# A gated linear attention with two expert stages: scores by row halves of the array, the state's decay on ScalarE, other warm-up matmuls

## The chip, the cores and the metric

The kernel runs on one NeuronCore of a Trainium2 chip. The metric is device time in microseconds (us), the median over runs of the same kernel. The engines are named as the profile names them: PE is TensorE's matmul part and PEld its weight loads, DVE is VectorE, ACT is ScalarE, POOL is GpSimd, and SP issues most of the DMAs. All of these run their own instruction streams in order and wait for each other through semaphores.

## The reference

Three stages follow one another. The change lies in the first; the other two are a top-2 mixture of experts and a gated unit on 3,072 tokens of width 384.

```python
# q, k, v, alpha: (B, H, S, D) = (4, 8, 768, 48)
for t in range(S):
    state = alpha[:, :, t, :, None] * state + einsum('bhd,bhe->bhde', k[:, :, t], v[:, :, t])
    y[:, :, t] = einsum('bhd,bhde->bhe', q[:, :, t], state)
x = y.transpose(0, 2, 1, 3).reshape(B * S, H * D)
x = moe(x)      # gate + noise, two best of 8 experts, relu(x @ w1) @ w2, weighted sum
x = glu(x)      # (sigmoid(x @ w_gate) * (x @ w_val)) @ w_out
```

## The kernel before, in words

**Attention** (`attention`, lines 24 to 235) cuts the sequence into 6 chunks of 128 steps and the 8 heads into 4 pairs. That gives 24 units, one chunk of one pair of heads each (`units[u] = (chunk, pair)`), for all 4 batch entries at once. In an operand of a unit the first head of the pair lies on partitions 0 to 47 and the second on 64 to 111, so that a tile has 112 rows; its 512 columns are 4 batch entries times 128 steps. A unit goes through these steps:

- `load` brings alpha, k and q of the unit in one DMA into one of four slots `ur` (line 57, 675.5 KB).
- `st_T` makes two running products of alpha by scans on DVE (`pd`, line 96, and its inverse from the chunk's end `gi`, line 98), after ACT has put the first column in place (line 95) and with a reciprocal between them (line 97). POOL then multiplies q by `pd` in place (line 107) and k by `gi` into `kt` (line 101). ACT copies the two heads' q into `q2` (line 110), where each head has its own 512 columns and the other head's rows hold zeros.
- `st_S` computes the scores of both heads with one matmul per batch entry: 112 rows, 256 columns, the zeros in `q2` keeping the heads apart (line 124). DVE applies the causal mask in two pieces into `am` (line 126).
- `st_K` transposes `kt` on PE (line 136).
- `st_Y` adds q times the state (line 148) and the masked scores times v (line 152) into `y`; each head has its own half of the array's columns there.
- `st_U` computes the update of the state into the PSUM tile `uu` (line 167); DVE adds it to the state `st` (line 170) and multiplies the sum by the chunk's total decay (line 171).
- `st_R` transposes the result back (line 179) and, after the fourth pair of a chunk, computes gate logits (line 186, 32 matmul records) and calls the **router** of that chunk: some thirty small DVE instructions with five matmuls into the PSUM tile `rk` (lines 271 to 326), then two tables (lines 329 to 346).

The loop (lines 217 to 234) issues in iteration u the scores of unit u+1, the outputs and the update of unit u, the scans of unit u+3 and the way back of unit u-1. A scheduler that works with its own estimates orders the instructions on each engine within these dependences; the order is fixed when the kernel runs. PSUM has eight banks here: `sc` two, `tr` two, and one each for `y`, `uu`, `rk` and the table.

Eight matmuls on the identity (line 198) run before the first operands arrive. After attention come the experts (lines 452 to 500) and the gated unit (lines 691 to 762), whose products are triples of float32r matmuls (lines 414 to 416). The weights of expert 0 are loaded during attention.

## Time and profile before

| | |
|---|---|
| median of 3 runs | 1150.58 us (1149.78 to 1151.04) |
| span of the profiled execution | 1151.6 us |
| PE busy | 1100.0 us (96%) |
| DVE busy | 493.5 us (43%) |
| ACT busy | 365.5 us (32%) |
| POOL busy | 341.7 us (30%) |
| first matmul of the experts | 195.85 us into the span |

The page gives the profiled execution's own time as its span, 1151.6 us, 1.0 us above the median of the timed runs. Attention fills the first 196 us of it. The busy shares in the table are averages over the whole span and hide that the stages differ: the page's row of 40 slices and the view by windows show each stage apart.

### The profile page before, as it was taken

Reading aid. Unit: us, or ns where it says so; the run is one execution under the profiler, and the core shown is the slowest. Engines: PE = TensorE matmul, PEld = TensorE weight load, DVE = VectorE, ACT = ScalarE, POOL = GpSimd, SP = SyncE. Lnnn points to the kernel's source line nnn. Section 1 sums busy time; section 2 is a strip of 40 time slices with the busy share of each in tenths; the row PEclk is TensorE's granted clock in tenths of the full one; section 3 lists DMA queues with packets and bytes.
Section 4 is the critical chain, followed back from the end, with each engine's and each line's share of the span. In section 5 each row is a group of like instructions: output and inputs, shape, how many; then the busy total and the mean of one; then the engine's idle time right before and its main releaser. Section 6 shows DMA issues by size and latency. Waiting matters only on the chain. (4 is left out here: it accounts for less than half of the span.)

```text
span 1151.6 us, 17338 instructions
## 1 busy us (share of the span) xinstructions
PE 1100.0 (96%) x6950; PEld 1047.7 (91%) x6950; DVE 493.5 (43%) x1042; ACT 365.5 (32%) x737; POOL 341.7 (30%) x284
## 2 busy tenths in 40 slices
PE   6898879999999999999999889899999999999998
PEld 5777668999999999999999878799999999999998
DVE  8889896422222222222224779451414141413131
ACT  3443433424242424242322334221313132313131
POOL 5534451634343433333321556440202020100000
PEclk8999889999999999999999989899999999999999
DMA  9845522433333333333332554230101010000000
GB/s 240 223 148 155 165 80 77 148 93 107 91 106 89 100 95 99 96 98 97 100 93 79 172 165 134 71 97 14 49 15 48 14 49 14 28 18 4 21 1 21
DMA packets 40293, 101.25 MB, mean 88 GB/s; under 512 B 5601, under 2 KB 19329, under 8 KB 40209
## 3 DMA queue, kind: packets, MB, share of 16 engines
q1 hardware_dynamic: 33680, 80.44, 23.8%
q0 software_dynamic: 6528, 19.67, 5.8%
q8 instruction: 55, 0.90, 0.3%
q14 instruction: 30, 0.24, 0.1%
HBM read 80.42 MB, written 19.66 MB: 87 GB/s over the span
## 5 line engine op out<-in xcount | busy, mean ns | idle before, releaser
L414 PE MATMUL pg<-x2h,whi 128*128 128x384 f32 x576 | 195.1, 339 | 4.0 <-DVE sg L739 2.8
L415 PE MATMUL pg<-x2l,whi 128*128 128x384 f32 x576 | 194.9, 338 | 0.0
L416 PE MATMUL pg<-x2h,wlo 128*128 128x384 f32 x576 | 194.0, 337 | 0.0
L473 DVE SCALAR_TENSOR_TENSOR h<-ph,h 128x384 fp32r<-128x384 f32 x192 | 79.7, 442 | 258.7 <-ACT h L470 258.6
L369 POOL TENSOR_TENSOR wlo<-raw,whi 128x768 fp32r<-128x768 f32 x64 | 117.5, 1843 | 123.7 <-ACT whi L368 123.4
L416 PE MATMUL ph<-xh,wlo 128*128 128x384 f32 (+1 forms) x384 | 136.2, 355 | 0.0
L415 PE MATMUL ph<-xl,whi 128*128 128x384 f32 (+1 forms) x384 | 135.9, 354 | 0.0
L414 PE MATMUL ph<-xh,whi 128*128 128x384 f32 (+1 forms) x384 | 135.8, 354 | 0.0
L414 PE MATMUL py<-whi,h 128*128 128x384 f32 x384 | 132.3, 344 | 0.0
L470 ACT ACTIVATE h<-ph 128x448 fp32r<-128x448 f32 (+1 forms) x128 | 66.2, 518 | 207.6 <-PE ph L416 207.5
L415 PE MATMUL py<-wlo,h 128*128 128x384 f32 x384 | 128.7, 335 | 0.0
L416 PE MATMUL py<-whi,h 128*128 128x384 f32 x384 | 116.1, 335 | 0.0
L414 PEld LDWEIGHTS pg<-x2h,whi 128*128 128x128 f32 x576 | 109.3, 190 | 5.6 <-DVE sg L739 4.1
L711 POOL DMA_INDIRECT grow<-yd,row x48 | 46.9, 977 | 222.0 <-PE pt L722 174.8
L415 PEld LDWEIGHTS pg<-x2l,whi 128*128 128x128 f32 x576 | 109.4, 190 | 0.0
L416 PEld LDWEIGHTS pg<-x2h,wlo 128*128 128x128 f32 x576 | 109.3, 190 | 0.0
L368 ACT ACTIVATE gh<-sg 128x384 fp32r<-128x384 f32 x96 | 50.5, 526 | 162.2 <-DVE sg L739 162.2
L414 PE MATMUL po<-whi,gh 128*128 128x384 f32 x288 | 97.0, 339 | 4.0 <-issue 2.1
L415 PE MATMUL po<-wlo,gh 128*128 128x384 f32 x288 | 97.1, 338 | 0.2 <-POOL wlo L369 0.2
L739 DVE TENSOR_TENSOR sg<-sg,pg 128x384 f32<-128x384 f32 x96 | 52.9, 551 | 102.4 <-PE pg L416 101.5
L416 PE MATMUL po<-whi,gl 128*128 128x384 f32 x288 | 96.8, 337 | 0.0
L435 POOL DMA_INDIRECT xrow<-xd,idx x56 | 53.2, 949 | 137.0 <-PE pt L446 110.0
(168 smaller groups left out, 1885.6 us busy)
## 6 DMA issues: line engine op xcount, KB each, us to landing
ur<-in_uh_dram SPq DMA_DIRECT2D x23, 675.5 KB, 6.1
raw<-in_w1h_dram SPq DMA_DIRECT2D x32, 384.0 KB, 3.4
raw<-in_w2h_dram SPq DMA_DIRECT2D x32, 384.0 KB, 3.1
yd<-yrow SPq DMA_DIRECT2D x48, 192.0 KB, 1.9
xv<-in_vh_dram SPq DMA_DIRECT2D x6, 768.0 KB, 6.9
xd<-xr SPq DMA_DIRECT2D x6, 768.0 KB, 5.7
raw<-in_wgh_dram SPq DMA_DIRECT2D x12, 384.0 KB, 3.3
raw<-in_wvh_dram SPq DMA_DIRECT2D x12, 384.0 KB, 3.4
```

The costliest lines, as they stand in the source:

```text
L368: a = nc.scalar.activation(hi, src, AF.Copy)
L369: b = e.tensor_tensor(lo, src, hi.bitcast(FT), op=OP.subtract)
L414: nc.tensor.matmul(out, wh, mh, start=first, stop=False)
L415: nc.tensor.matmul(out, wh, ml, start=False, stop=False)
L416: nc.tensor.matmul(out, wl, mh, start=False, stop=last)
L435: nc.gpsimd.indirect_dma_start(out=x[:n], out_offset=None, in_=src, in_offset=bass.IndirectOffsetOnAxis(ap=g.idx[:n, e, a:a + 1], axis=0))
L470: a = nc.scalar.activation(h[:, :tot], p[:, :tot], AF.Relu)
L473: b = nc.vector.scalar_tensor_tensor(h[:, lo:lo + j - i], p[:, i:j], 0.0, h[:, i:j].bitcast(FT), op0=OP.max, op1=OP.subtract)
L711: nc.gpsimd.indirect_dma_start(out=r, out_offset=None, in_=src, in_offset=bass.IndirectOffsetOnAxis(ap=g.row[:, n, k:k + 1], axis=0))
L739: nc.vector.tensor_tensor(sg, sg, pp[1], op=OP.mult)
```

## The change

The scores of a unit are now eight matmuls instead of four. Each takes one head's 48 rows, which lie in the lower or the upper half of the array's rows, and 128 columns; the two heads alternate and write two PSUM tiles `s[0]` and `s[1]` in different banks (`sc` has three banks now). They read q where POOL left it, in the unit's `ur` slot, so that the copies into `q2` remain only for chunks after the first, where `st_Y` needs them, and unit 0's q is multiplied on DVE in place. A slot can be loaded again only when the scores of its unit are done; in the program text `load(u + 5)` therefore stands behind the scores of unit u+1. `am` has the heads outside the batch entries. The eighth bank comes from the router: `rk` now shares the one bank of `uu`, and the plan of the overflow (line 528) has a PSUM pool of its own. The decay of the state is four ACT instructions, one for each batch entry, with the decay as a factor per partition. The warm-up is six matmuls on the identity and thirteen on a tile of zeros in float32r, 4,480 columns together; DVE fills the tile of zeros. Comments and docstrings are gone.

```diff
@@ attention
-        nc.gpsimd.memset(q2[0], 0.0)
-        nc.gpsimd.memset(q2[1], 0.0)
...
+                qr = col(UQ)
                 if u == 0:
-                    return [e.tensor_tensor(flat(q2[0][:, j])[64 * j:64 * j + D, cs], col(UQ)[64 * j:64 * j + D],
-                                            flat(pd)[64 * j:64 * j + D, cs], op=OP.mult).ins
-                            for j, e in enumerate((nc.vector, nc.gpsimd))]
-                qr = col(UQ)
+                    return [nc.vector.tensor_tensor(qr, qr, flat(pd)[:, cs], op=OP.mult).ins]
                 q = nc.gpsimd.tensor_tensor(qr, qr, flat(pd), op=OP.mult)
-                for j in range(2):
-                    sl = slice(64 * j, 64 * j + D)
-                    nc.scalar.activation(flat(q2[u % 3][:, j])[sl], qr[sl], AF.Copy)
+                if units[u][0]:
+                    for j in range(2):
+                        sl = slice(64 * j, 64 * j + D)
+                        nc.scalar.activation(flat(q2[u % 3][:, j])[sl], qr[sl], AF.Copy)
...
         def st_S(u):
-            am = aw.tile([128, B, 2, C], FT, name="am", tag="am", bufs=2)
-            for h in range(2):
-                s = ps.tile([128, 2, 2, C], FT, name="sc", tag="sc", bufs=2)
-                for b in range(2):
-                    nc.tensor.matmul(s[:, b], KT[u][:, 2 * h + b, :], q2[u % 3][:RW, :, 2 * h + b, :],
-                                     start=True, stop=True)
-                k = nc.vector.tensor_tensor(am[:, 2 * h:2 * h + 2].rearrange("p b j t -> p (b j) t"),
-                                            s.rearrange("p b j t -> p (b j) t"), mask_b, op=OP.mult)
+            am = aw.tile([128, 2, B, C], FT, name="am", tag="am", bufs=2)
+            qt = ur[u % LB][:, UQ:UQ + BC].rearrange("p (b t) -> p b t", b=B)
+            s = [ps.tile([128, B, C], FT, name="sc", tag="sc", bufs=3) for j in range(2)]
+            for b in range(B):
+                for j in range(2):
+                    sl = slice(64 * j, 64 * j + D)
+                    nc.tensor.matmul(s[j][:, b], KT[u][sl, b, :], qt[sl, b, :], start=True, stop=True)
+            for j in range(2):
+                k = nc.vector.tensor_tensor(am[:, j], s[j], mask_b, op=OP.mult)
...
             nc.vector.tensor_tensor(s, s, o[:RW], op=OP.add)
-            nc.vector.tensor_tensor(s, s, PD[u][:, :, C - 1:C].to_broadcast([RW, B, D]), op=OP.mult)
+            for b in range(B):
+                nc.scalar.activation(s[:, b], s[:, b], AF.Copy, scale=PD[u][:, b, C - 1:C])
...
-        warm = ps.tile([128, C], FT, name="warm", tag="tr", bufs=2)
-        for _ in range(8):
-            nc.tensor.matmul(warm, ident, ident, start=True, stop=True)
+        warm = ps.tile([128, 512], FT, name="warm", tag="tr", bufs=2)
+        for _ in range(6):
+            nc.tensor.matmul(warm[:, :128], ident, ident, start=True, stop=True)
+        zero = aw.tile([128, 512], FR, name="zero", tag="am", bufs=2)
+        nc.vector.memset(zero.bitcast(FT), 0.0)
+        for w in (384, 256, 256, 256, 256, 256, 320, 320, 320, 320, 512, 512, 512):
+            nc.tensor.matmul(warm[:, :w], zero[:, :128], zero[:, :w], start=True, stop=True)
...
         st_S(0)
+        load(4)
         st_K(0, first)
-        load(4)
...
+            if u + 1 < n:
+                st_S(u + 1)
             load(u + 5)
             if p == 1 and c:
                 load_v(c + 1)
-            if u + 1 < n:
-                st_S(u + 1)
@@ router (and the same in router_fix)
-    rk = g.rps.tile([128, B, E], FT, name="rk", tag="rk", bufs=1)
+    rk = g.aps.tile([128, B, E], FT, name="rk", tag="uu", bufs=1)
```

The scheduler lays the engines' streams out anew. Three places matter below. In the rows, `st_139` to `st_142` are the states of pairs 0 to 3, and `ur_126` to `ur_129` the four slots.

On DVE, in the first chunk, the state's add and decay of units 0 and 1 stood between the scans like this before:

```order
L98 SCALAR_TENSOR_TENSOR gi<-ur_128,d_137 112x512
L170 TENSOR_TENSOR st_139<-st_139,uu 112x192
L96 SCALAR_TENSOR_TENSOR pd<-ur_129,d_136 112x512
L126 TENSOR_TENSOR am<-sc,mask 128x512
L171 TENSOR_TENSOR st_139<-st_139,pd 112x192
L97 RECIPROCAL d_138<-pd 112x4
L170 TENSOR_TENSOR st_140<-st_140,uu 112x192
L98 SCALAR_TENSOR_TENSOR gi<-ur_129,d_138 112x512
L171 TENSOR_TENSOR st_140<-st_140,pd 112x192
```

Now DVE keeps only the adds there:

```order
L96 SCALAR_TENSOR_TENSOR gi<-ur_128,d_137 112x512
L95 RECIPROCAL d_138<-pd 112x4
L168 TENSOR_TENSOR st_139<-st_139,uu 112x192
L96 SCALAR_TENSOR_TENSOR gi<-ur_129,d_138 112x512
L168 TENSOR_TENSOR st_140<-st_140,uu 112x192
```

and ACT has the decays, in order with the copies that other engines wait for:

```order
L153 ACTIVATE xt<-y 128x512
L170 ACTIVATE st_139<-st_139,pd 112x48 x4
L372 ACTIVATE whi<-raw 128x768
L153 ACTIVATE xt<-y 128x512
L372 ACTIVATE whi<-raw 128x768
L170 ACTIVATE st_140<-st_140,pd 112x48 x4
```

The decays have left DVE, and on ACT they stand between the copies of `y` and the splits of the weights.

On DVE, where the router of the first chunk runs, the adds of units 6 and 7 (pairs 2 and 3 of the second chunk) stood among the router's instructions, one of them ahead of the two that read `rk`:

```order
L170 TENSOR_TENSOR st_141<-st_141,uu 112x192
L326 TENSOR_TENSOR wts<-w,wts 128x4
L171 TENSOR_TENSOR st_141<-st_141,pd 112x192
L96 SCALAR_TENSOR_TENSOR pd<-ur_128,d_135 112x512
...
L311 TENSOR_TENSOR m<-m,rk 128x32 x2
L313 TENSOR_REDUCE rank<-m 128x8
...
L170 TENSOR_TENSOR st_142<-st_142,uu 112x192
```

Now, since `uu` and `rk` are one bank, the add of unit 5 (pair 1) already comes behind the readers of `rk`:

```order
L315 TENSOR_TENSOR m<-m,rk 128x32 x2
L317 TENSOR_REDUCE rank<-m 128x8
...
L346 TENSOR_TENSOR ohh<-ohe,ids 128x224
L168 TENSOR_TENSOR st_140<-st_140,uu 112x192
L344 TENSOR_TENSOR ohe<-codes,code 128x224
L346 TENSOR_TENSOR ohh<-ohe,ids 128x224
L94 SCALAR_TENSOR_TENSOR pd<-ur_127,d_136 112x512
```

The updates of units 5, 6 and 7, pairs 1 to 3 of the second chunk, now all stand behind the readers of `rk`; before, only that of unit 7 did.

On SP the loads of units 4 and 5 stood between those of expert 0's weights:

```order
L395 DMA raw<-in_w1h_dram 128x768
L57 DMA ur_126<-in_uh_dram 112x1544
L395 DMA raw<-in_w1h_dram 128x768 x2
L57 DMA ur_127<-in_uh_dram 112x1544
```

Now all three weight loads go first:

```order
L399 DMA raw<-in_w1h_dram 128x768 x3
L57 DMA ur_126<-in_uh_dram 112x1544
L57 DMA ur_127<-in_uh_dram 112x1544
```

Two weight loads have moved ahead of unit 4's operands.

## Rows read from the trace of the kernel before

**Rows 1.** The page, busy tenths of PE and DVE in 40 slices of the span.
```profile
PE   6898879999999999999999889899999999999998
...
DVE  8889896422222222222224779451414141413131
```
**Rows 2.** By windows of the attention stage: us, busy time (instructions) of each engine, PEclk, DMA.
```profile
core 0: us, PE busy (x) PEld busy (x) DVE busy (x) ACT busy (x) POOL busy (x), PEclk, DMA share, GB/s
15.00:50.00 35.00, 30.17 (x278) 23.10 (x278) 33.02 (x44) 17.73 (x38) 18.99 (x14) 0.90 0.97 248
50.00:78.00 28.00, 25.85 (x301) 21.72 (x298) 24.88 (x64) 12.11 (x27) 9.21 (x7) 0.98 0.49 144
78.00:110.00 32.00, 27.36 (x299) 23.48 (x300) 28.99 (x66) 14.33 (x31) 14.46 (x11) 0.91 0.51 158
110.00:145.00 35.00, 28.98 (x313) 24.79 (x307) 31.96 (x67) 15.03 (x33) 18.00 (x13) 0.90 0.55 170
145.00:175.00 30.00, 22.81 (x255) 19.24 (x254) 29.64 (x67) 9.25 (x21) 14.38 (x10) 0.89 0.26 77
```
**Rows 3.** DVE by line and form, 15 to 178 us: busy us, mean ns | idle before, releaser.
```profile
L96 DVE TENSOR_TENSOR_SCAN pd<-ur,d 112x512 f32<-112x512 f32 x22 | 30.3, 1379 | 1.8 <-ACT d L95 1.1
L126 DVE TENSOR_TENSOR am<-sc,mask 128x512 f32<-128x512 f32 x43 | 28.5, 669 | 1.0 <-PE sc L124 0.7
L171 DVE TENSOR_TENSOR st<-st,pd 112x192 f32<-112x192 f32 x20 | 16.4, 818 | 0.3
L170 DVE TENSOR_TENSOR st<-st,uu 112x192 f32<-112x192 f32 x20 | 6.8, 340 | 6.9 <-PE uu L167 6.9
```
**Rows 4.** Line 171 alone: ns min/median/max, first and last start.
```profile
L171 DVE TENSOR_TENSOR st<-st,pd x20: 326/360/2823, 23.6 to 172.9; 112x192 f32<-112x192 f32 x20
```
**Rows 5.** DVE in order of time, the longest decay and the longest scan: start us, us.
```profile
143.34 2.82 DVE L171 TENSOR_TENSOR st<-st,pd 112x192 f32<-112x192 f32 x1
150.42 3.74 DVE L96 TENSOR_TENSOR_SCAN pd<-ur,d 112x512 f32<-112x512 f32 x1
```
**Rows 6.** PE in order of time in one unit at the full clock: start us, us.
```profile
65.19 0.60 PE L179 MATMUL tr<-ident,xt 128*128 128x128 f32 x4
65.63 1.89 PE L124 MATMUL sc<-q,kt 112*128 112x256 f32 x8
67.45 0.44 PE L148 MATMUL y<-q,st 128*64 128x128 f32 x4
67.72 0.39 PE L152 MATMUL y<-am,xv 128*64 128x128 f32 x4
67.94 0.39 PE L148 MATMUL y<-q,st 128*64 128x128 f32 x4
```
**Rows 7.** ACT by line, 0 to 330 us: small copies, busy us, mean ns.
```profile
L95 ACT ACTIVATE d<-ur 112x4 f32<-112x4 f32 (+1 forms) x25 | 5.1, 207 | 45.7 <-DVE pd L96 16.8 <-DMA ur<-in_uh_dram 15.5 <-issue 13.2
...
L190 ACT ACTIVATE ls<-tr 128x128 f32<-128x128 f32 x6 | 1.6, 272 | 10.8 <-PE tr L186 10.8
```
**Rows 8.** PE in order of time at the start: start us, us [idle before, releaser].
```profile
2.07 3.41 PE L198 MATMUL warm<-ident 128*128 128x128 f32 x16 [2.07 <-POOL ident masks.py:199]
7.78 1.48 PE L124 MATMUL sc<-q,kt 112*128 112x256 f32 x4 [2.30 <-DVE kt L101]
...
12.30 2.05 PE L124 MATMUL sc<-q,kt 112*128 112x256 f32 x4 [2.66 <-DVE d L97]
```
**Rows 9.** ACT in order of time at the start: first columns of units 1 and 2.
```profile
10.37 0.21 ACT L95 ACTIVATE d<-ur 112x4 f32<-112x4 f32 x1 [7.07 <-DMA ur<-in_uh_dram]
...
16.79 0.21 ACT L95 ACTIVATE d<-ur 112x4 f32<-112x4 f32 x1 [1.49 <-DMA ur<-in_uh_dram]
```
**Rows 10.** By windows at the start (columns as in Rows 2).
```profile
10.00:15.00 5.00, 2.42 (x7) 1.65 (x8) 4.36 (x6) 1.71 (x4) 3.08 (x6) 0.50 1.03 254
15.00:20.00 5.00, 5.00 (x35) 3.76 (x36) 3.74 (x6) 1.63 (x5) 1.29 (x2) 0.64 1.04 260
```
**Rows 11.** PE in order of time where the experts begin.
```profile
178.63 1.99 PE L124 MATMUL sc<-q,kt 112*128 112x256 f32 x8
...
195.85 0.42 PE L414 MATMUL ph<-xh,whi 128*128 128x384 f32 x1
196.11 0.34 PE L415 MATMUL ph<-xl,whi 128*128 128x384 f32 x1
196.28 0.34 PE L416 MATMUL ph<-xh,wlo 128*128 128x384 f32 x1
```
**Rows 12.** Loads of line 57, from issue to landing.
```profile
DMA to landing us min/median/max: 4.6/6.1/15.1
```

More of the change, by code (lines that the diff above doesn't have):

```diff
@@ L33, in attention @@
             tc.tile_pool(name="aps", bufs=1, space=PSUM) as ps:
-        ident = g.ident
+        ident, g.aps = g.ident, ps
         LB = 4
@@ L151, in st_Y @@
                     h0 = b * HD + (2 * p + j) * D
-                    nc.tensor.matmul(y[64 * j:64 * j + 64, b], vt[:, h0:h0 + 64], AM[u][:, b, j, :],
+                    nc.tensor.matmul(y[64 * j:64 * j + 64, b], vt[:, h0:h0 + 64], AM[u][:, j, b, :],
                                      start=not c, stop=True, skip_group_check=True)
@@ L205, in attention @@
         with tc.issue_after(g.after_T):
-            nc.gpsimd.memset(q2[2], 0.0)
+            for t in q2:
+                nc.gpsimd.memset(t, 0.0)
             for p in range(NP):
@@ L352, in router_fix @@
     E = g.E
-    pc = g.rps.tile([128, E], FT, name="pc", tag="rk", bufs=1)
+    pc = g.aps.tile([128, E], FT, name="pc", tag="uu", bufs=1)
     nc.tensor.matmul(pc, g.ones, g.run, start=True, stop=True)
@@ L526, in overflow_plan @@
     TT = lambda *a, **k: nc.vector.tensor_tensor(*a, **k)
-    pc = g.rps.tile([128, E], FT, name="oc", tag="rk", bufs=1)
-    nc.tensor.matmul(pc, g.ones, g.run, start=True, stop=True)
     cnt = t("cnt", [128, E])
-    TT(cnt, pc, g.roff, op=OP.add)
+    with tc.tile_pool(name="ops", bufs=1, space=PSUM) as ops:
+        pc = ops.tile([128, E], FT, name="oc")
+        nc.tensor.matmul(pc, g.ones, g.run, start=True, stop=True)
+        TT(cnt, pc, g.roff, op=OP.add)
     one = t("one", [128, E])
```

## The prediction

> **What bounds the kernel now.** I read the page's slices first, to see which engine is full in which stage. PE is full from the seventh slice on, in the experts and the gated unit; in the first six, 173 us, DVE is the fuller of the two almost throughout [rows 1]. The change touches the attention stage and the router in it, so what it is worth is read there. The windows of that stage give, from 15 to 175 us, 33.02 + 24.88 + 28.99 + 31.96 + 29.64 = 148.5 us of DVE in 160 us, 93%. PE has 30.17 + 25.85 + 27.36 + 28.98 + 22.81 = 135.2 us there, 84%, part of it at a granted clock that drops to half (means of 0.89 to 0.98). ACT has 68.4 us, 43% [rows 2]. So DVE sets the pace and PE follows closely; ACT has room. DVE's own idle time confirms it: before its longest groups it waits 1.8 us and 1.0 us in total, and only the add of the state's update, line 170, has a real wait, 6.9 us in 20 instructions, for PE [rows 3].
>
> Behind the attention stage the experts' products begin at 195.85 us and follow each other every 0.17 us [rows 11], with PE full up to slice 20 [rows 1]. Nothing there can take up time that attention gives back, so what is saved before 196 us comes off the end, one for one. The profiled span of 1151.6 us stands 1.0 us above the median of the runs shown; I take the sum off the median, 1150.58 us. About 0.2%, 2.3 us, is what a measurement can tell from no change.
>
> **The change, part by part.**
>
> *The decay leaves DVE.* Line 171 costs DVE 16.4 us in 20 instructions, 818 ns each [rows 3]. The median is only 360 ns, the longest 2,823 ns [rows 4]: the same operation on the same shape, so the rest is waiting inside the instruction while something else is being served. The part that surely goes is 20 x 0.36 = 7.2 us. The other 16.4 - 7.2 = 9.2 us are stalls, and a stall can pass to the next instruction. A scan has stalled for 3.74 us where its mean is 1.38 us [rows 3, 5], so scans are not safe from it. I take half of the stalls as gone: 7.2 + 4.6 = **11.8 us gained**, with 7.2 and 16.4 us as the ends.
>
> *The decay arrives on ACT.* It is four instructions of 112 x 48 a unit, 80 in all. The nearest ACT rows are a copy of 112 x 4 at 207 ns and one of 128 x 128 at 272 ns [rows 7]; between them I take 240 ns, 80 x 0.24 = 19 us. ACT has 160 - 68.4 = 91.6 us idle in the stage [rows 2], and three units' copies into `q2` leave it, so in total it fits. But ACT works in order: a decay waits for DVE's add, which waits for PE's update, and the first columns for the scans and the copies of `y` queue behind it. DVE waits for such a first column when it is late, 1.1 us in the stage now [rows 3]. I take 1 us lost; the ends are 0 and a wait like those of line 170, 6.9 us.
>
> *The scores.* Now a unit's scores start at 65.63 us and the next group at 67.45 us: 1.82 us for eight records [rows 6]. The array is already split by columns in `y`: there four records, two matmuls of 128 columns for each half, start every 0.22 us (67.72 to 67.94) [rows 6]. One such matmul alone streams half as many columns as a score matmul now, which is 1.82 / 4 = 0.455 us, so about 0.23 us; two in 0.22 us means that the halves really run together. If the row halves do likewise, a unit's scores take 4 x 0.22 = 0.9 us. If they stream one after the other, 8 x 0.23 = 1.8 us, as now. In between stands the weight load: each score matmul loads 128 columns anew, and the transposes at 65.19 us, which also load 128 columns each, need 0.44 us for four, 0.11 us a load, for operands that stream little [rows 6]. Sixteen loads (two records a matmul) in a row would be 1.76 us, in pairs 0.88 us. I take the middle of 0.9 and 1.8, 1.3 us, so 0.5 us of PE a unit.
>
> The Trainium skill (TensorE: Matmul & The Clock Gate, section LDWEIGHTS) has the load's time go by columns alone, not by rows, and lets it overlap with matmuls of another row group; that agrees with 0.11 us for 128 columns, and no run here shows whether two loads overlap. By serial loads the scores would gain 0.06 us a unit, and the sum below would lose its PE term.
>
> In the DVE-bound stretch the 22 units' 0.5 us, 11 us of PE, are hidden behind DVE and I count them as nothing. They do keep PE below DVE: without them PE's 135.2 us would stand against DVE's 148.5 - 11.8 = 136.7 us. From 175 to 196 us PE is the bound, with the last two units' scores in it, the first of them at 178.63 us and 1.99 us long [rows 11]. There 2 x 0.65 = **1.3 us gained**, with 0 and 2.2 us as the ends.
>
> *q read from the slot.* A slot is now free only when the unit's scores are done, not when ACT has copied q. A load takes 6.1 us from issue to landing in the median, 15.1 us at most [rows 12]. Scans run two units or more ahead of scores, and a slot serves every fourth unit, so two units' time is left, about 2 x 160 / 22 = 14.5 us. That covers the median. At the start DMA is full (0.97 of it, 248 GB/s, 15 to 50 us [rows 2]), and two weight loads of 0.39 MB now go ahead of unit 4's load: 0.79 MB / 248 GB/s = 3.2 us later. I take **1 us lost** for units 4 to 8, with 0 and 3.2 us as the ends. Later loads are hidden.
>
> *`rk` in the bank of `uu`.* Unit 5's update now waits until DVE has read the ranks. DVE still has the rest of the router and a table to do between the two, as the order shows, and PE's outputs of units 6 to 8 stand ahead of that update on PE. I cost it at nothing; what hides it is that DVE work. Without the cover each of five rounds would cost one wait like the present ones of line 170, which I bound below among the rivals.
>
> *The start.* Warm-up before: 16 records in 3.41 us from 2.07 us, then PE idles 2.30 us until DVE has `kt` at 7.78 us [rows 8]. Now it is 12 records, 2.6 us, and 4,480 columns; a 384-column product takes 0.17 us at the full clock [rows 11], so 2.0 us, or 4.0 us at half. It ends between 6.7 and 8.7 us, against 7.78 us. The second half of the first scores stands at 12.30 us, behind DVE's chain for unit 1 [rows 8], whose operands land only at 10.37 us, and unit 2's at 16.79 us [rows 9]. PE ran at a granted 0.50 and 0.64 in these ten microseconds [rows 10]; a fuller warm-up may raise that, but DMA sets the pace there. The memset of the zeros (nearest: 112 x 512) and the q product on DVE also end in that wait. Nothing, with 1 us either way.
>
> The sum: -11.8 + 1 + 1 - 1.3 = -11.1 us, 1150.6 - 11.1 = **1139.5 us**. Most of the ends together give 1134 to 1146 us for this case.
>
> **The rivals.**
>
> *Both engines give way (more gain).* If the stalls vanish with line 171 (16.4 us) and the faster scores also end DVE's waits for PE (6.9 us), with 1.3 us at the end: 1150.6 - 24.6 = 1126 us; half way there 1132 us. For it: PE and DVE are both near full. Against: a scan stalls as well [rows 5].
>
> *A wait takes the place.* The bank shared by `rk` and `uu`, or a decay late on ACT, holds DVE up once or twice a chunk. The price: 6.9 us of waits before line 170 fell mostly on few instructions; a wait of about 2 us a unit in the 5 chunks that update, 5 to 6 of them, is 10 to 12 us and eats the gain: 1139.5 + 10 to 12, with 1.5 us of play 1148 to 1153 us. For it: the updates of units 5 to 7 are bunched behind the router. Against: DVE has work in between.
>
> *The row halves do not run together (slower).* Streams and loads then add up: 8 x 0.23 + 16 x 0.11 = 3.6 us a unit against 1.82 us. PE would gain 22 x 1.8 = 39 us of work in a stretch of 160 us that has 135.2 us of it [rows 2]. It decides from 160 - 135.2 = 25 us on, 1.1 us a unit. Beyond that PE is the bound: 39 - 25 = 14 us, and 4 us for the last two units, 1168 us; with loads partly hidden 1154 us. For it: no row here shows row halves. Against: column halves do run together.
> The Trainium skill (TensorEngine Tiling (Array Packing), section Tiling Modes, Key Properties) says that a change of tiling mode drains TensorE, which speaks against this change, since scores now have a mode of their own. In the trace the first group of `y` behind the scores takes 0.27 us and the next 0.22 us, so a drain of about 0.05 us; that agrees in kind and is small.
>
> **How the numbers follow.** Forecast 0.62, more gain 0.12, a wait in its place 0.12, slower 0.14. Faster by over 0.2%: 0.62 + 0.12 and a sixth of the third case, 0.76; within 0.2%: the rest of that case, 0.10; slower 0.14. The range 1128 to 1151 us holds the forecast, most of the greater gain and half of the third case, about 0.8.
>
> **What would show it.** Right: line 170 on ACT at some 240 ns, no multiply of the state on DVE, DVE still over 90% busy up to some 165 us, scores near 1.3 us a unit, the first expert product at some 185 us. Wrong: DVE idle before adds or masks with PE or ACT as the releaser, score groups of 3 us, first columns waiting for DMA, or a first expert product at 196 us or later.

## The result and the profile after

The changed kernel takes 1164.91 us (1163.57 to 1166.47), the kernel before, timed beside it, 1150.5 us (1149.78 to 1151.04): a ratio of 1.0116 [1.0094, 1.0139] (of the times, with its 95% interval in brackets, here and below), 14 us slower. I had forecast 1139.5 us and a range up to 1151 us; sign and range are both wrong.

The profiled execution has a span of 1162.6 us, 11 us more than the profiled one of before; the timed medians lie 14 us apart. The page's slices of PE and DVE answer to [rows 1], and the granted clock is shown beside them:

```profile
PE   7898788899999999999999889899999999999998
...
DVE  7788896422222222222223869642414141413131
...
PEclk8789888999999999999999999999999999999999
```

The experts begin at 206.84 us, 11 us later than in [rows 11], and the rest of the span behind them is as long as before (955.8 us either way). So what the two profiles differ in happens in attention:

```profile
206.84 0.42 PE L418 MATMUL ph<-xh,whi 128*128 128x384 f32 x1
207.10 0.34 PE L419 MATMUL ph<-xl,whi 128*128 128x384 f32 x1
```

The windows of that stage, columns as in [rows 2]:

```profile
15.00:50.00 35.00, 29.90 (x285) 26.37 (x286) 28.34 (x36) 16.98 (x45) 20.53 (x18) 0.70 0.77 210
50.00:78.00 28.00, 26.29 (x326) 22.86 (x328) 19.93 (x58) 14.23 (x41) 6.41 (x5) 0.93 0.43 124
78.00:110.00 32.00, 28.55 (x353) 24.49 (x352) 28.22 (x63) 17.60 (x48) 14.60 (x10) 0.93 0.48 147
110.00:145.00 35.00, 28.52 (x315) 24.75 (x314) 30.51 (x62) 19.30 (x48) 21.56 (x13) 0.84 0.55 169
145.00:175.00 30.00, 26.36 (x288) 22.06 (x287) 29.72 (x53) 13.95 (x32) 23.79 (x14) 0.86 0.48 149
```

DVE is busy for 136.7 us of these 160 us instead of 148.5 us; PE for 139.6 instead of 135.2 us although its scores are shorter, at a lower clock in four of the five windows. (The windows are the same times, not the same work: the changed kernel has 11 us more of attention behind them.) DVE by line and form, 15 to 178 us, and the decay's line on ACT alone, which answer to [rows 3, 4]:

```profile
L96 DVE TENSOR_TENSOR_SCAN gi<-ur,d 112x512 f32<-112x512 f32 x22 | 43.7, 1986 | 1.1
L94 DVE TENSOR_TENSOR_SCAN pd<-ur,d 112x512 f32<-112x512 f32 x22 | 37.0, 1682 | 4.3 <-ACT d L93 3.5 <-ACT st L170 0.8
L125 DVE TENSOR_TENSOR am<-sc,mask 128x512 f32<-128x512 f32 x42 | 27.5, 674 | 9.3 <-PE sc L123 7.8 <-PE y L150 1.4
```
```profile
L170 ACT ACTIVATE st<-st,pd x80: 317/319/336, 24.0 to 189.3; 112x48 f32<-112x48 f32 x80
```

The decay's 16.4 us have left DVE, and its scans have grown by as much, from 64.0 us (30.3 for `pd` [rows 3] and 33.7 for `gi`) to 80.7 us. That is not one passing into the other: where the decay alone is moved, the scans grow far less, to 70.8 us in decay_only, and from 69.8 to 72.5 us between own_bank_decay_back and after_own_bank (all below). DVE also waits 9.3 us before masks, where it was 1.0 us. The scores themselves did what they should, a unit in 1.09 us at the full clock against 1.82 us [rows 6]; PE in order of time:

```profile
87.89 1.16 PE L123 MATMUL sc<-ur,kt 48*128 48x128 f32 x16
88.98 0.33 PE L191 MATMUL tr<-ident,ls 128*128 128x128 f32 x1
```

### The profile page after: what moved, and what is told of

It reads as the page before. It is cut to its first block, busy times and chain, and to the rows that moved or that the text cites. A ratio compares the mean times of both kernels' runs of the same rounds, so it can differ in the third digit from the quotient of the medians.

```text
span 1162.6 us, 17796 instructions
## 1 busy us (share of the span) xinstructions
PE 1109.5 (95%) x7151; PEld 1060.3 (91%) x7151; DVE 485.6 (42%) x1023; ACT 380.5 (33%) x811; POOL 349.9 (30%) x282
## 3 DMA queue, kind: packets, MB, share of 16 engines
q1 hardware_dynamic: 33680, 80.44, 23.1%
## 5 line engine op out<-in xcount | busy, mean ns | idle before, releaser
L373 POOL TENSOR_TENSOR wlo<-raw,whi 128x768 fp32r<-128x768 f32 x64 | 121.1, 1899 | 126.4 <-ACT whi L372 126.0
L418 PE MATMUL ph<-xh,whi 128*128 128x384 f32 (+1 forms) x384 | 136.7, 357 | 0.0
```

Of the source, the lines that this page charges most:

```text
L373: b = e.tensor_tensor(lo, src, hi.bitcast(FT), op=OP.subtract)
L418: nc.tensor.matmul(out, wh, mh, start=first, stop=False)
```

## The experiments

Two figures are worked out for every kernel from windows of 1 us, from 10 us to the first product of the experts. *Idle* is the time in which PE was not busy. *Slow* is PE's busy time times one minus the granted clock: what its work took beyond what it takes at the full clock. They carry an error of a few us, since some matmul records are missing. Four profiles (decay_only, no_decay, scores_split, rows_after_start) hold no record of the clock before 21.4, 18.5, 17.2 and 21.2 us, and the windows print 1.00 there. Their matmuls say otherwise: four score matmuls of 112 rows and 256 columns take 2.04 us in this stretch of rows_after_start, as at 0.50 in the kernel before [rows 8, 10], and 1.13 us later at the full clock.

```profile
12.78 2.04 PE L125 MATMUL sc<-q,kt 112*128 112x256 f32 x4 [2.57 <-DVE d L97]
```

So this stretch is counted at half the clock for these four. The ratio is to the kernel before, timed beside each (its medians there: 1150.5 to 1151.7 us).

| kernel | us | ratio [95%] | experts begin | slow | idle |
|---|---|---|---|---|---|
| before | 1150.5 | 1 | 195.85 | 13.2 | 27.4 |
| after | 1164.9 | 1.0116 [1.0094, 1.0139] | 206.84 | 27.2 | 30.1 |
| bank_only | 1164.8 | 1.0115 [1.0098, 1.0132] | 209.10 | 11.7 | 39.2 |
| rows_only | 1153.7 | 1.0028 [1.0014, 1.0042] | 200.58 | 30.6 | 28.2 |
| decay_only | 1152.3 | 1.0014 [1.0004, 1.0025] | 196.40 | 14.4 | 26.5 |
| after_own_bank | 1152.0 | 1.0002 [0.9989, 1.0014] | 194.63 | 19.7 | 27.9 |
| after_decay_back | 1172.9 | 1.0189 [1.0171, 1.0207] | 215.72 | 29.1 | 37.2 |
| own_bank_decay_back | 1152.0 | 1.0001 [0.9991, 1.0011] | 193.64 | 23.6 | 24.5 |
| after_pd6 | 1161.0 | 1.0081 [1.0058, 1.0104] | 203.47 | 22.3 | 24.6 |
| after_router_later | 1160.5 | 1.0085 [1.0062, 1.0108] | 201.89 | 27.1 | 25.8 |
| no_decay | 1155.2 | 1.0024 [1.0003, 1.0045] | 196.35 | 17.9 | 25.3 |
| own_bank_no_decay | 1163.5 | 1.0088 [1.0062, 1.0114] | 203.63 | 28.1 | 32.1 |
| own_bank_pd6 | 1161.4 | 1.0094 [1.0070, 1.0117] | 200.92 | 27.5 | 28.1 |
| decay_only_pd6 | 1151.6 | 1.0008 [0.9993, 1.0023] | 198.95 | 12.0 | 32.5 |
| own_bank_kt_dve | 1151.3 | 1.0001 [0.9987, 1.0016] | 195.70 | 28.7 | 23.1 |
| own_bank_fill2 | 1155.8 | 1.0041 [1.0018, 1.0064] | 198.86 | 19.4 | 24.5 |
| own_bank_fill4 | 1176.6 | 1.0217 [1.0179, 1.0255] | 215.66 | 20.1 | 30.7 |
| own_bank_decay_back_fill2 | 1167.4 | 1.0138 [1.0115, 1.0161] | 208.74 | 23.9 | 27.6 |
| scores_split | 1152.8 | 1.0017 [1.0007, 1.0026] | 193.85 | 10.8 | 27.3 |
| rows_after_start | 1154.5 | 1.0021 [1.0008, 1.0035] | 198.72 | 24.9 | 29.0 |

### The parts alone, and without one part

**rows_only**: the kernel before with `st_S` by row halves (and `am` ordered by head for it), q from `q2`, `rk` in its own bank. Here and below `...` stands for code that is left out.

```diff
-                    nc.tensor.matmul(s[:, b], KT[u][:, 2 * h + b, :], q2[u % 3][:RW, :, 2 * h + b, :], ...)
+                    nc.tensor.matmul(s[j][:, b], KT[u][sl, b, :], q2[u % 3][sl, j, b, :], ...)
```


> The kernel before with the scores by row halves alone: q still read from the copies in q2, masks by head, two banks for sc, the router's own bank, decay on DVE, old warm-up. In its order on DVE 23 of 45 neighbouring scans have no mask between them (13 before, 25 after). Order theory (scans that stand side by side meet POOL's products and get longer; 33 of 46 met one after the change, 20 before): most of the loss is here already, 1157 to 1165 us, over 28 scans that meet a product. Bank theory (rk in the bank of uu makes the wait): no loss, 1140 to 1150 us. Decay theory (the decay comes late on ACT): no loss, 1140 to 1150 us.

**decay_only**: the kernel before with the four ACT instructions in place of line 171.

> The kernel before with the decay on ACT alone. Order on DVE: 13 of 45 scan pairs without a mask, as before. Order theory: the decay's stalls go only in part to scans, 1142 to 1149 us, about 20 scans that meet a product. Bank theory: the same, 1140 to 1149 us. Decay theory: the loss is here, 1155 to 1165 us, with DVE or PE waiting for line 171 on ACT.

**after_decay_back**: the changed kernel with line 171 back on DVE.

> The changed kernel with the decay back on DVE. 25 of 45 scan pairs without a mask, as after. Order theory: not faster than after, 1162 to 1172 us. Bank theory: as after or slower, 1162 to 1172 us. Decay theory: back to 1145 to 1152 us.

**after_own_bank**: the changed kernel with two banks for `sc` instead of three, and the third given to `rk`, `pc` and `oc`.

```diff
-    rk = g.aps.tile([128, B, E], FT, name="rk", tag="uu", bufs=1)
+    rk = g.rps.tile([128, B, E], FT, name="rk", tag="rk", bufs=1)
-            s = [ps.tile([128, B, C], FT, name="sc", tag="sc", bufs=3) for j in range(2)]
+            s = [ps.tile([128, B, C], FT, name="sc", tag="sc", bufs=2) for j in range(2)]
```


> The changed kernel with the router's own bank again and therefore two banks for sc. 18 of 45 scan pairs without a mask. Order theory: between the two, 1152 to 1160 us, since the order lies between the two. Bank theory: the whole loss goes, 1138 to 1150 us. Decay theory: little change, 1158 to 1166 us.

Measured: 1153.7, 1152.3, 1172.9 and 1152.0 us. The bank is the one part that costs much: 12.9 us between after and after_own_bank. But after_own_bank only comes back to the kernel before and brings none of the gain that the bank theory left over, and decay_only gains nothing either. rows_only loses 3 us, less than the order theory gave. The decay theory falls: decay_only takes 1152.3 us and not 1155 to 1165, and putting the decay back makes the changed kernel slower. rows_only, decay_only and after_decay_back lie outside every range that was given, after_own_bank at the lower end of the order theory's. No part gains anything by itself. The decay's move is worth 8.0 us where the bank is shared (1172.9 to 1164.9) and nothing where it is not (own_bank_decay_back, below).

**bank_only** puts `rk` and `pc` into the bank of `uu` in the kernel before and changes nothing else.

```diff
-    rk = g.rps.tile([128, B, E], FT, name="rk", tag="rk", bufs=1)
+    rk = g.aps.tile([128, B, E], FT, name="rk", tag="uu", bufs=1)
```


> The kernel before with rk and the table's counts in the bank of uu and nothing else changed: the decay stays on DVE, the scores as they were. Chain theory: the shared bank costs by itself what it cost in the changed kernel, about 13 us, 1159 to 1166 us, with scans standing behind the routers. Rival, it only costs because the decay on ACT comes behind it, or because PE and DVE changed their order around the new scores: under 4 us, 1149 to 1155 us.

1164.8 us: the shared bank costs 14 us alone, with the decay and the scores as they were. PE's slow time does not rise (11.7 us); its idle time does, by 11.8 us. So this part is a wait, as the chain theory has it; the next section follows it. In the changed kernel the same bank shows up in other columns: against after_own_bank the idle time is 2.2 us higher and the slow time 7.5 us. Nor do the parts add up: after_decay_back, which differs from bank_only in the row halves, q's product, the loads and the warm-up, takes 8 us more than it. No run says which of these costs that.

### The way of the bank's cost

The next four pieces are DVE in order of time around the first router (start us, us, then the idle time before and its releaser). They show scans (not all of them), the state's add and decay, and the first reader of `rk`; `...` stands for what is left out. The kernel before:

```profile
47.27 1.23 DVE L96 TENSOR_TENSOR_SCAN pd<-ur,d 112x512 f32<-112x512 f32 x1
...
54.04 0.36 DVE L170 TENSOR_TENSOR st<-st,uu 112x192 f32<-112x192 f32 x1 [2.53 <-PE uu L167]
54.43 0.36 DVE L171 TENSOR_TENSOR st<-st,pd 112x192 f32<-112x192 f32 x1
54.88 1.22 DVE L96 TENSOR_TENSOR_SCAN pd<-ur,d 112x512 f32<-112x512 f32 x1
...
61.69 1.22 DVE L96 TENSOR_TENSOR_SCAN pd<-ur,d 112x512 f32<-112x512 f32 x1
...
66.77 0.28 DVE L311 TENSOR_TENSOR m<-m,rk 128x32 f32<-128x32 f32 x2
```

bank_only:

```profile
48.74 1.72 DVE L98 TENSOR_TENSOR_SCAN gi<-ur,d 112x512 f32<-112x512 f32 x1
...
61.03 0.28 DVE L311 TENSOR_TENSOR m<-m,rk 128x32 f32<-128x32 f32 x2
...
64.26 0.35 DVE L170 TENSOR_TENSOR st<-st,uu 112x192 f32<-112x192 f32 x1 [0.60 <-PE uu L167]
64.83 0.35 DVE L171 TENSOR_TENSOR st<-st,pd 112x192 f32<-112x192 f32 x1
65.40 1.22 DVE L96 TENSOR_TENSOR_SCAN pd<-ur,d 112x512 f32<-112x512 f32 x1
```

The changed kernel:

```profile
55.10 1.66 DVE L96 TENSOR_TENSOR_SCAN gi<-ur,d 112x512 f32<-112x512 f32 x1
...
65.77 0.28 DVE L315 TENSOR_TENSOR m<-m,rk 128x32 f32<-128x32 f32 x2
...
68.55 0.36 DVE L168 TENSOR_TENSOR st<-st,uu 112x192 f32<-112x192 f32 x1 [0.16 <-PE uu L165]
...
70.44 1.23 DVE L94 TENSOR_TENSOR_SCAN pd<-ur,d 112x512 f32<-112x512 f32 x1 [0.81 <-ACT st L170]
71.70 0.18 DVE L95 RECIPROCAL d<-pd 112x4 f32<-112x4 f32 x1
71.99 2.11 DVE L96 TENSOR_TENSOR_SCAN gi<-ur,d 112x512 f32<-112x512 f32 x1
```

after_own_bank:

```profile
56.08 0.35 DVE L168 TENSOR_TENSOR st<-st,uu 112x192 f32<-112x192 f32 x1
...
57.77 1.23 DVE L94 TENSOR_TENSOR_SCAN pd<-ur,d 112x512 f32<-112x512 f32 x1 [0.46 <-ACT st L170]
...
60.30 0.27 DVE L315 TENSOR_TENSOR m<-m,rk 128x32 f32<-128x32 f32 x2
...
64.80 1.22 DVE L94 TENSOR_TENSOR_SCAN pd<-ur,d 112x512 f32<-112x512 f32 x1
```

Before, the add of unit 5 comes at 54.04 us, and scans run beside the router, at 54.88 and 61.69 us; in after_own_bank it is much the same. With the shared bank, in bank_only and in the changed kernel, unit 5's add comes only behind the reader of `rk`, at 64.26 and 68.55 us, and no scan runs for 14.9 and 13.7 us. It is the same at the second and the third router: 12.2 and 13.7 us without a scan in bank_only, 12.5 and 15.0 us in the changed kernel, while the longest such stretch is 6.8 us before and 6.7 us in after_own_bank. The bank goes from tile to tile in the order of the program text, and there the router of the first chunk stands ahead of unit 5's update. A scan into `pd` needs a buffer; there are four, and the scan of unit 9 gets that of unit 5, which is free when unit 5's decay has read it. So the chain is: router, update, decay, buffer, scan. POOL, which waits for the scans, stands idle for 13.58 us meanwhile in the changed kernel:

```profile
71.75 1.27 POOL L103 TENSOR_TENSOR ur<-ur,pd 112x512 f32<-112x512 f32 x1 [13.58 <-DVE pd L94]
```

Two runs change this chain and leave the bank shared. **after_pd6** gives `pd` six buffers:

```diff
-            pd = aw.tile([RW, B, C], FT, name="pd", tag="pd", bufs=4)
+            pd = aw.tile([RW, B, C], FT, name="pd", tag="pd", bufs=6)
```


> The changed kernel with six buffers for the running product pd instead of four; rk still shares the bank of uu. Chain theory (router holds the update, the update holds the decay, the decay holds the pd buffer, and the scans of four units later stand behind it): with two more buffers the scans no longer stand behind the router, POOL's idle stretch of 13.6 us beside the first router is gone, and most of the 13 us comes back: 1148 to 1156 us. Rival, the waits for the bank hurt by themselves (PE's updates, the adds, the order of the router's instructions, of masks and scans): no more than a third comes back, 1160 to 1166 us.

**after_router_later** issues a chunk's router one unit later in the text, behind the next unit's update (the list `late` holds it until then):

```diff
...
             st_U(u)
+            if late:
+                on_round(*late.pop())
...
```


> The changed kernel, rk still in the bank of uu, but the router of a chunk stands one unit later in the program text, behind the update of the next unit (not for the last chunk and one other). The bank goes to rk and uu in the order of the text, so the update of the second pair of the next chunk no longer waits for the router. Theory that the 13 us are the updates which stand behind the router (three a round): one of three is taken out of three of the rounds, so 3 to 6 us come back, 1158 to 1162 us. Rival, the loss comes from the bank's turn as such or from the bunched scans whatever is ahead: 1163 us or more.

They measured 1161.0 and 1160.5 us, about 4 us back each. after_router_later is as expected: with one of three updates ahead of the router in three of the rounds, about a third of the loss is gone. after_pd6 falls to the rival by its time, no more than a third comes back. But its trace shows the chain still whole: two more scans into `pd` pass beside the first router (51.99 and 58.77 us), and then the scan of unit 11, whose buffer is now that of unit 5, stands behind the same decay.

```profile
60.31 2.27 DVE L96 TENSOR_TENSOR_SCAN gi<-ur,d 112x512 f32<-112x512 f32 x1
...
73.33 1.23 DVE L94 TENSOR_TENSOR_SCAN pd<-ur,d 112x512 f32<-112x512 f32 x1 [0.35 <-ACT st L170]
```

At the three routers 10.8, 13.0 and 16.6 us pass without a scan there, and 11.2, 12.2 and 11.0 us in after_router_later. So it is shown that the shared bank costs 13 to 14 us and that updates behind the router cost time (three of the twelve moved ahead, 4 us back). That the `pd` buffers are the whole way from the late update to the end is argued from the order: no run has enough buffers to take that link out.

### What the decay is worth

**no_decay** leaves the decay out altogether, in the kernel before (a constant factor in the copy `km` keeps the state small); **own_bank_no_decay** does so in after_own_bank, where the decay's lines are those on ACT.

```diff
-            nc.vector.tensor_tensor(s, s, PD[u][:, :, C - 1:C].to_broadcast([RW, B, D]), op=OP.mult)
-            nc.scalar.activation(km, o[:, :, :RW], AF.Copy)
+            nc.scalar.activation(km, o[:, :, :RW], AF.Copy, scale=1e-6)
```


> The kernel before without the state's decay on any engine (left out: the multiply of the state by the chunk's decay; in its place the copy into km carries a constant factor 1e-6, about the mean decay of a chunk, so that the state stays small). This is the most that taking the decay off DVE can ever give, with no late decay on ACT. My prediction's premise, DVE's time in this stage comes off the end one for one: 1134 to 1144 us (7.2 to 16.4 us faster). Rival, the stage's pace comes from the chain through scans, POOL's products, scores, masks, outputs and router, not from DVE's fullness: 1147 to 1152 us.

> The changed kernel with rk in its own bank and without any decay (left out as in no_decay). With the decay on ACT this kernel took 1152.0 us, and DVE waited 9.0 us for ACT to release pd. Theory that this late release takes the gain: 1141 to 1147 us. Rival, scans that stall beside POOL's products and the order of the work take it: 1149 to 1153 us.

**own_bank_decay_back** is after_own_bank with line 171 back on DVE.

> The changed kernel with rk in its own bank and the decay back on DVE: what is left of the change is the row halves, the q product in the slot, the order of the loads and the warm-up. It completes the table bank times decay. If the decay's move is worth as much with its own bank as with the shared one (8 us): 1158 to 1162 us. If it is worth only what it was alone (nothing): 1151 to 1155 us, near rows_only's 1153.7 us.

**own_bank_pd6** and **decay_only_pd6** are after_own_bank and decay_only with six `pd` buffers.

> The changed kernel with rk in a bank of its own (scores in two banks) and six buffers for pd. Before this run, with four buffers, DVE waited 9.0 us in six scans for ACT's decay to release pd. Theory that the late decay on ACT takes what its leaving DVE gives: these waits go and the time falls by 4 to 9 us, 1143 to 1148 us, faster than the kernel before. Rival, DVE is not what limits any more (PE at a lower clock, or scans that stall beside POOL's products): the waits move elsewhere and the time stays within 2 us of 1152 us.

> The kernel before with the decay on ACT alone and six buffers for pd. In the run with four buffers, 1152.3 us, DVE waited 6.8 us in eight scans for ACT to release pd. Late-decay theory: 1144 to 1149 us. Rival, PE as the limit beside DVE: 1150 to 1153 us, with PE busier and DVE's idle time put down to PE in place of ACT.

This is what fells my main term. With no decay on any engine the kernel before takes 1155.2 us, not 1134 to 1144 us, and not even the rival's 1147 to 1152. own_bank_decay_back equals after_own_bank (1152.0 us both), and decay_only_pd6, 1151.6 us, falls to its rival by the time, though PE is not busier there, as the rival had it (156.4 us up to the experts, 159.9 in decay_only). Where `rk` has its own bank, moving the decay, putting it back and leaving it out all give the same time or a longer one. What becomes of the time on DVE is seen in no_decay, 15 to 178 us, first before, then no_decay (columns as in [rows 2]), then what DVE waits for there (us in total, times, longest):

```profile
15.00:178.00 163.00, 138.17 (x1465) 114.93 (x1466) 148.66 (x305) 70.22 (x151) 75.05 (x53) 0.92 0.56 160
```
```profile
15.00:178.00 163.00, 139.53 (x1457) 118.11 (x1454) 141.99 (x285) 69.93 (x150) 81.50 (x53) 0.91 0.53 158
DVE am L126 <- PE sc L124: 5.7, 6, 1.3
DVE pd L96 <- ACT d L95: 3.5, 5, 1.1
DVE gi L98 <- POOL kt L101: 2.8, 4, 0.9
```

Of the 16.4 us DVE gives back 6.7; the rest returns as longer scans and router instructions. And the 6.7 us become waiting, for PE, ACT and POOL; in the kernel before DVE waits 0.7 us for these scores and 1.1 us for the first columns [rows 3]. The late release of `pd` by ACT is real, in after_own_bank:

```profile
DVE pd L94 <- ACT st L170: 9.0, 6, 2.5
```

(us in total, times, longest), but taking it away with more buffers did not help: own_bank_pd6 has no such wait and is 9 us slower, own_bank_no_decay 11 us; both lie outside what either theory gave. So the theory of the late release finds no support. In own_bank_no_decay and own_bank_pd6 the scans may run further ahead, and PE's slow time is 8 us higher than in after_own_bank; why is not settled. Every edit here also makes the scheduler lay the streams out anew, and no run holds the order fixed: 9 us for two more buffers shows how much that can move, so a time that an edit failed to save is weaker evidence than the waits in its trace.

### What a scan waits for

In the rows of after above, the scan at 70.44 us takes 1.23 us, and the one at 71.99 us takes 2.11 us. POOL's product ran from 71.75 to 73.02 us: 1.03 us of waiting for its end and 1.2 us of scan are about that. Counted in the timelines of DVE and POOL, a scan that overlaps a product on POOL (of attention, or of the experts' weights, `wlo`) by less than 0.3 us takes 1.22 us on average, in after as in before; one that overlaps more takes 2.07 us in after (33 of 46 scans) and 1.77 us in before (20 of 46). The masks never stall (654 to 693 ns for all 48 of after); they read PSUM and one tensor in SBUF. The Trainium skill (SBUF — State Buffer, section Who interferes with whom) states that DVE and GpSimd share a port pair as an exclusive lock; the trace agrees for scans, which read two SBUF tensors, 2.07 us against 1.22 us.

**own_bank_kt_dve** puts the products `kt` of all units on DVE.

```diff
-                e = nc.vector if u < 2 else nc.gpsimd
+                e = nc.vector
```


> The changed kernel with rk in its own bank and the product kt of all units on DVE instead of POOL. DVE gets 20 products of some 0.69 us more, 14 us. Contention theory (a scan takes 1.2 us alone and about 2 us beside a product on POOL): scans beside POOL's products fall from 24 to about 12 of 46, the scans' total falls by about 10 us and pays for most of it: 1150 to 1156 us with a mean scan under 1.45 us. Rival, scans are long for another reason: their mean stays at 1.65 us and the time rises by the products, 1160 to 1168 us.

DVE by line and form, 15 to 178 us:

```profile
L96 DVE TENSOR_TENSOR_SCAN gi<-ur,d 112x512 f32<-112x512 f32 x22 | 44.7, 2032 | 0.2
L94 DVE TENSOR_TENSOR_SCAN pd<-ur,d 112x512 f32<-112x512 f32 x22 | 28.8, 1309 | 1.9 <-issue 1.7
L99 DVE TENSOR_TENSOR kt<-ur,gi 112x512 f32<-112x512 f32 x22 | 17.2, 781 | 0.2
```

The time, 1151.3 us, is inside the contention theory's range, but not for its reason: the mean scan is 1.67 us, not under 1.45. 14 scans meet work on POOL instead of 24, yet take longer (2.71 us), and the scans' sum stays at 73.5 us against 72.5 us. The timelines say why. Ten of the 14 meet only the product of q, and these take 2.07 us on average, as in after. The other four meet splits of the experts' weights on POOL (`wlo`, 128 x 768), one or two in a row, and take 2.58, 4.01, 4.85 and 5.77 us, 17.2 us together; the four that meet splits in after_own_bank take 10.3 us. The longest:

```profile
57.72 5.77 DVE L96 TENSOR_TENSOR_SCAN gi<-ur,d 112x512 f32<-112x512 f32 x1
```
```profile
57.60 1.27 POOL L103 TENSOR_TENSOR ur<-ur,pd 112x512 f32<-112x512 f32 x1 [4.56 <-PE uu L165]
58.83 3.58 POOL L373 TENSOR_TENSOR wlo<-raw,whi 128x768 fp32r<-128x768 f32 x2
```

The contention is as the theory has it, and half of the scans are free of it; what it left out are the splits, which now follow the product of q at once and hold scans just as well. DVE is busy for 149.0 us from 15 to 178 us against 142.6 in after_own_bank, so 16.5 us of products more are 6.3 us net, and they cost nothing in total, as the 6.7 us less of no_decay gained nothing.

### The clock of TensorE

In the table the six kernels with the old scores have 10.8 to 17.9 us of slow time, and the fourteen with row halves 19.4 to 30.6 us. Every timed execution has its mean granted clock on record too: the medians are 0.978 to 0.982 for the six, and 0.962 to 0.972 for the fourteen. Row halves save PE 8 to 13 us of work at the full clock (145.2 us before, 131.8 in rows_only, 137.0 in after_own_bank, each to the experts), and 6.5 to 17 us go into a lower clock.

**scores_split** cuts each old score matmul into two of 128 columns, on all 112 rows; **rows_after_start** is rows_only with the old scores for units 0 to 4.

```diff
-                    nc.tensor.matmul(s[:, b], KT[u][:, 2 * h + b, :], q2[u % 3][:RW, :, 2 * h + b, :],
...
+                    for j in range(2):
+                        nc.tensor.matmul(s[:, b, j], KT[u][:, 2 * h + b, :], q2[u % 3][:RW, j, 2 * h + b, :],
...
```


> The kernel before with each score matmul (112 rows, 256 columns) cut into two of 128 columns, still on all 112 rows with the zeros in q2. It has the row halves' number of matmuls and weight loads without the row halves. If the half-filled rows are what keeps TensorE's clock at half for longer: PE's slow loss stays at 10 to 15 us as in the five kernels with the old scores, 1149 to 1154 us. Rival, it comes from the many short matmuls or from the new order: slow loss of 19 us or more, or over 1156 us.

> rows_only (1153.7 us, slow loss 30.6 us), with the scores of units 0 to 4 in the old form of 112 rows. In rows_only TensorE stays at half clock up to about 36 us though PE is full from 16 us on; in the kernel before it is at the full clock from 18.6 us. If row halves keep the clock down: it is up at about 19 us again, the slow loss falls to 18 to 24 us, and the time to 1145 to 1151 us, which would beat the kernel before if below 1148. Rival, the slow start there is chance of the order: no change, 1152 to 1156 us.

One window of rows_only, then of rows_after_start (columns as in [rows 2]):

```profile
20.00:26.00 6.00, 6.00 (x52) 5.67 (x52) 5.14 (x8) 1.84 (x4) 5.25 (x3) 0.50 1.04 266
```
```profile
20.00:26.00 6.00, 6.00 (x58) 4.71 (x58) 6.00 (x8) 2.27 (x4) 2.54 (x2) 1.00 1.05 267
```

PE is full in both, at 1.2 GHz with row halves and, from 21.2 us on, at 2.4 GHz with the old scores. In rows_only the clock stays at 0.50 from 26 to 36 us as well, with PE busy for 8.06 of 10 us. scores_split has as many matmuls as the row halves and the lowest slow time of all, 10.8 us; over its ten executions the median of the mean clock is 0.982, as before, and 0.966 in rows_only. So the clock goes with the row halves, not with the number of matmuls; that is shown. What it is about them is not. But rows_after_start, with 6 us less slow time than rows_only, takes 1154.5 us: its slow time, 24.9 us, stays just above what was expected, and its gain is not there. It is no test of the clock alone: the old scores of five units are also 3 us more work for PE, so that PE's busy time up to the experts only falls from 162.4 to 159.7 us. The clock is where the saved work went; no run raised it without adding work.

**own_bank_fill2**, **own_bank_fill4** and **own_bank_decay_back_fill2** put two or four idle matmuls ahead of each unit's scores, on the tile of zeros, which is kept for them. The edit, simplified:

```diff
+            for _ in range(2):
+                nc.tensor.matmul(s[0].rearrange("p b t -> p (b t)"), g.zero[:, :128], g.zero, start=True, stop=True)
```


> The changed kernel with rk in its own bank and, ahead of each unit's scores, two idle matmuls of 512 columns on zeros, written into the score tile and overwritten. Clock theory (what the row halves save on PE goes back into TensorE's clock, which stands at half for 20 us of PE's time more than needed in this kernel, 13 us in the kernel before): PE's slow loss falls from 19.7 to under 13 us, and although 48 matmuls cost 10 us of PE at 0.21 us each, the time does not rise by that: 1146 to 1153 us. Rival, the pace is PE's work itself or the chain through DVE and POOL, and the clock follows from it: 1156 to 1164 us.

> The same with four idle matmuls a unit, 20 us of PE at the full clock. Clock theory: slow loss under 8 us, time 1148 to 1158 us. Rival: about 20 us more than 1152 us, 1166 to 1174 us.

> own_bank_decay_back (1152.0 us; slow loss 23.6 us, idle 24.5 us of PE up to the experts) with two idle matmuls a unit. Clock theory: slow loss under 14 us, 1143 to 1151 us, and it would be the candidate that beats both kernels. Rival as for own_bank_fill2: 1156 to 1164 us.

1155.8, 1176.6 and 1167.4 us, with slow times of 19.4, 20.1 and 23.9 us, as without them. The idle matmuls do not lower the slow time, and they hide in part at best: 4, 25 and 15 us more than without them for 10, 20 and 10 us of added PE work. The clock theory asked for a slow time under 13, 8 and 14 us, so it falls; the rival's ranges are not hit either (one time lies just below, two above). PE's time does count, then.

## Why the prediction was wrong

- **"`rk` in the bank of `uu` ... I cost it at nothing; what hides it is that DVE work."** This step failed. What I put at nothing costs 13 to 14 us (bank_only, after_own_bank). The order that I showed had the sign of it: three adds behind the readers of `rk`. I looked at who works meanwhile (DVE has a router to run) and not at what the late update holds up in turn: the decay, the `pd` buffer, the scans, POOL, and in the trace 12.5 to 15.0 us without a scan at each of three routers. My second rival had the cause and nearly the size, 10 to 12 us, at a chance of 0.12, but as waits of 2 us a unit and set against a gain that does not exist.
- **"What is saved before 196 us comes off the end, one for one", and "DVE sets the pace".** Wrong, and it carried the whole gain. no_decay takes all of line 171 away, which leaves DVE 6.7 us less busy, and gains nothing; own_bank_kt_dve adds 16.5 us of products, 6.3 us net, and loses nothing. The 93% of [rows 2] held 9.2 us of stalls in line 171, at 1.22 us a scan 10 us in the scans (64.0 - 44 x 1.22), and 10 us in two router instructions (lines 315 and 322 take 1423 and 1520 ns on average in the kernel before, 165 and 164 ns in after), so it did not say that DVE was full.
- **The decay leaves DVE, 11.8 us.** The sure 7.2 us and half the stalls were to go. Line 171 is gone, and my warning that a stall can pass on was right: where the decay alone is moved (decay_only), the scans grow by 6.8 us and DVE's busy time from 15 to 178 us falls by 5.7 us, less than even the sure 7.2. But it was not the share that failed: none of what DVE gave back came off the end.
- **The decay on ACT, 240 ns.** It takes 319 ns, 25.5 us in all. It fitted, as I said; DVE waits 0.8 us for it in the changed kernel, 9.0 us in after_own_bank, against my 1 us.
- **The scores, 1.3 us a unit.** 1.09 us, better than my middle. The halves run together, and so do their weight loads: 16 loads in a row would be 1.76 us by my price. The Trainium skill (TensorE: Matmul & The Clock Gate, section LDWEIGHTS) lets a load run ahead of matmuls where the row groups do not conflict; here the 16 loads of a unit start in pairs, one of each half, a pair every 0.11 us (87.89 to 88.67 us), so loads overlap with each other as well. My rival of halves that do not run together is refuted, though the time fell into its range: right sign, wrong reason. What I did not think of is that PE's clock answers to the form of the scores.
- **q from the slot, and the start.** Unit 4's first scan starts at 30.39 us against 27.81 us, but after_own_bank, which has the same loads in the text, has it at 28.39 us and loses nothing. With the new warm-up the clock is 0.83 from 10 to 15 us against 0.50 [rows 10], and down again afterwards (0.50 from 15 to 20 us, 0.64 before); the second half of the first scores came at 12.39 us, before at 12.30 us [rows 8]. Nothing, as forecast for the start; no run takes these two out alone.

Two of my signs of being wrong came true: DVE waits before masks for PE (7.8 us, where it was 0.7), and the first expert product is later than 196 us.

What sets the 186 us of attention once the bank is put right stays open. PE idles for 23 to 32 us there in nearly every kernel; less work on PE, on DVE or on both does not shorten it, more on PE lengthens it. No version ran that beats the kernel before; after_own_bank, own_bank_decay_back, own_bank_kt_dve and decay_only_pd6 equal it.

## What to carry to other kernels

When two tiles come to share a buffer, follow the one that now waits through all that it holds in turn; idle time that is covered on one engine can starve the next. Before an engine's busy time is counted as the pace, leave the work out once and time it: a stage of engines coupled by few buffers can have an engine that is 93% busy and still give nothing back, since part of the busy time is waiting inside instructions, and what is freed becomes waiting elsewhere.

## What the runs showed of the hardware

- Scores on the two halves of the array's rows overlapped, matmuls and weight loads (eight matmuls of 48 x 128 x 128 in f32 with 16 loads in 1.09 us; four of 112 x 256 took 1.82 us). But from 20 to 36 us TensorE was at 1.2 GHz with them (rows_only, busy for 6.00 of 6 and 8.06 of 10 us), where 112-row scores had it at 2.4 GHz from 21.2 us on (rows_after_start).
- With thirteen matmuls on zeros more at the start the clock was 0.83 in place of 0.50 from 10 to 15 us; two or four ahead of each unit's scores left the slow time as it was (19.4 and 20.1 us against 19.7).
- A scan that meets a product on POOL takes about 2 us in place of 1.22 us, and one that meets a product and two weight splits in a row took 5.77 us. With one of the two products moved to DVE, the splits came right behind the other one and the scans' sum stayed (73.5 us against 72.5).
